# The feed-forward down projection with moving weights in four column groups, row output on two queues, longer weight runs, and x on the second queue

## The chip, the core and the metric

The kernel runs on one core of one Trainium2 chip. The metric is the device time of one execution in microseconds (us); medians are over several executions. Each execution also leaves its span, from the first to the last instruction on the core, and one execution of each kernel is traced by the hardware profiler. Spans are printed to 0.1 us, so stage lengths that run to the end of the span are good to 0.05 us.

In the profile PE is TensorE (its matmuls; PEld its weight loads), DVE is VectorE, ACT ScalarE and SP SyncE. A q, as in SPq, marks what the engine's sequencer does, such as issuing a DMA. SBUF is the core's working memory, PSUM the memory that matmuls write to. A time "at clock 0.5" was taken while the granted TensorE clock was at half.

## The reference

Two tokens pass through one decoder layer: attention over the last 2048 positions of a cache with 32 heads of 192, then a gated feed-forward network. Nearly all bytes are the cache.

```python
x = A_x                                               # [2, 1, 640], bf16
h = x + attention(layernorm(x), k_cache, v_cache, wq, wo)   # 32 heads, window 2048, head size 192
n = layernorm(h)
h2 = h + (gelu(n @ w_gate) * (n @ w_up)) @ w_down     # w_gate, w_up [640, 1536], w_down [1536, 640]
```

## The kernel before

All big loads go through a ring of SBUF slots on SyncE's DMA queue, in the order of their use: K, V and the projections for 16 groups of heads (two pairs of K and V each), then w_gate, w_up and w_down. The parts that the change touches are these (cuts are marked):

```python
P.op("sp", lambda e: e.dma_start(xrow[0:2, :], A_x[:, 0, :]), W=["xrow"], dma="dx")   # x first, same queue
load_k(0)
# ... all other loads; the last ones are:
for key, w in (("wg", B_w_gate), ("wu", B_w_up)):
    load(key, 2 * NC5 * F, w.rearrange("(p c) f -> p c f", c=NC5), ...)
wd = B_w_down.rearrange("(f p) n -> p f n", p=128)            # runs of 640 bf16 = 1280 B
for i in range(3):
    load(("wd", i), 2 * 4 * D, wd[:, 4 * i:4 * i + 4, :], ...)

# ... attention; then
layernorm(hT, "hT", hnT, "hnT")                               # h is held transposed: [128, 5, 2]
# gate and up: weights stationary, two columns (the two tokens) move
ins = e.matmul(bank[:, 2 * f:2 * f + 2], lhsT=wv[:, c, 128 * f:128 * (f + 1)], rhs=hnT[:, c, :], ...)
# ... gelu on DVE and ACT, uT = gelu(gate) * up
# w_down: weights stationary with a stride of 5, two columns move, 3 x 20 matmuls
ins = e.matmul(m2[:, 2 * c:2 * c + 2], lhsT=wd[:, f, c:D:NC5], rhs=uT[:, 4 * i + f, :], ...)
dve(tt(yT[...], m2[...], hT[:, :, :], ALU.add), ...)          # y stays transposed
e.dma_start(out[:, 0, :].rearrange("b (p c) -> p b c", c=NC5), yT[:, :, :])   # 256 pieces of 10 B
```

## Time and profile before

| what | value |
|---|---|
| time | 305.16 us, median of 3 (304.79 to 305.4) |
| span of the traced run | 303.6 us |
| DMA rate while the cache streams | about 420 GB/s, engines 90% busy or more from slice 2 to 38 |
| output of the second layernorm ready (hnT) | 290.66 us |
| uT ready | 294.80 us |
| last w_down group may start | 297.92 us |
| output issued | 299.13 us, 4.47 us before the end of the span |

The first lines to read are three rows of the page's forty slices of the kernel before: the TensorE clock that was granted, the busy share of the DMA engines (both in tenths) and the rate.

```profile
PEclk9999979995798899798799999798579999998555
DMA  6999999999999999999999999999999999999980
GB/s 240 412 435 414 427 426 420 428 399 427 425 422 423 426 421 421 427 399 428 421 428 426 421 418 426 421 407 420 433 419 426 421 421 417 429 419 424 417 308 27
```

The middle of the kernel is bound by DMA and nothing in this change touches it. What can change is how soon the stream starts, and what follows its end. TensorE's clock is at half from the 38th slice on.

The end of the chain of waits of the kernel before (start, duration, what) says which work ended last:

```profile
274.65 23.22 DMA ring<-in_B_w_down_dram
297.88 0.04 issue
297.92 0.97 PE m L629 x20
298.90 0.02 issue
298.92 0.18 DVE yT L316
```

In this execution the last landing of w_down ended the kernel: PE waited for it, then did 20 matmuls, DVE added h, and the output left. The timeline of the same execution (start, duration, engine, line, operation, and in brackets the idle time before and what ended it) has the start and the final stages:

```profile
0.74 0.37 SPq L318 DMA_DIRECT2D xrow<-in_A_x_dram  x1
1.17 1.28 SPq L261 DMA_DIRECT2D ring<-in_A_k_cache_dram  x2
...
290.71 1.76 PE L606 MATMUL sps<-hnT,ring 128*128 128x2 bf16 x60 [0.85 <-DVE hnT L316]
292.75 1.76 PE L606 MATMUL ops<-hnT,ring 128*128 128x2 bf16 x60 [0.28 <-DMA ring<-in_B_w_up_dram]
294.62 0.18 DVE L316 TENSOR_TENSOR uT<-ops,ga 128x24 bf16<-128x24 f32 x1 [0.26 <-PE ops L606]
294.86 0.96 PE L629 MATMUL m<-uT,ring 128*128 128x2 bf16 x20 [0.35 <-DVE uT L316]
296.03 0.80 PE L629 MATMUL m<-uT,ring 128*128 128x2 bf16 x16 [0.21 <-DMA ring<-in_B_w_down_dram]
297.19 0.28 PE L629 MATMUL m<-uT,ring 128*128 128x2 bf16 x4 [0.37 <-issue]
297.92 0.96 PE L629 MATMUL m<-uT,ring 128*128 128x2 bf16 x20 [0.45 <-DMA ring<-in_B_w_down_dram]
299.13 0.39 SPq L637 DMA_DIRECT2D out_dram<-yT  x1
```

x's issue delays the first K by 0.43 us. Gate and up take 29 ns per matmul (1.76/60), the w_down matmuls 48 ns (0.96/20), all at clock 0.5.

### The profile page before, as it was taken

To read this page: it belongs to the slowest core of one execution; us is meant where nothing else is said; L and a number is where in the kernel's file an instruction comes from. 1 tells how busy PE (TensorE), PEld (TensorE's weight loads), DVE (VectorE), ACT (ScalarE), POOL (GpSimd) and SP (SyncE) were. 2 spreads that over 40 slices of the span, in tenths; PEclk is the share of its full clock that TensorE was granted. 3 is DMA by queue.
4 is the path that set the end of the run, shared out by engine and by line. 5 is a ranking of instruction groups with operands and counts; after the bars stand their busy time and mean duration, and the time that the engine had idled before them with its cause. 6 is when DMAs were issued, how large, how long until landed. Compare 5 with 4: busy or idle time off the path is not lost.

```text
span 303.6 us, 7058 instructions
## 1 busy us (share of the span) xinstructions
PE 235.6 (78%) x3169; PEld 190.1 (63%) x3169; DVE 130.5 (43%) x360; ACT 112.2 (37%) x138; POOL 3.2 (1%) x9
## 2 busy tenths in 40 slices
PE   2878798962999988791898979692799889796762
PEld 1737394932868675771867676671785858575662
DVE  5837263720345364341446454351252736453120
ACT  2336343630425263522336353432243644442000
POOL 4000000000000000000000000000000000000000
PEclk9999979995798899798799999798579999998555
DMA  6999999999999999999999999999999999999980
GB/s 240 412 435 414 427 426 420 428 399 427 425 422 423 426 421 421 427 399 428 421 428 426 421 418 426 421 407 420 433 419 426 421 421 417 429 419 424 417 308 27
DMA packets 16323, 122.76 MB, mean 404 GB/s; under 512 B 1698, under 2 KB 3236, under 8 KB 7844
## 3 DMA queue, kind: packets, MB, share of 16 engines
q1 hardware_dynamic: 16292, 122.30, 96.9%
q8 instruction: 25, 0.41, 0.6%
q14 instruction: 6, 0.05, 0.0%
HBM read 122.29 MB, written 0.00 MB: 403 GB/s over the span
## 4 chain that ended last, share of the span: by engine, by line
DMA 57%; PE 31%; SPq 5%; DVE 3%; ACT 1%; issue 1%
DMA ring<-in_A_k_cache_dram 49%; PE tps L427 19%; DMA ring<-in_B_w_down_dram 8%; SPq L261 5%; PE m L541 3%; PE sps L489 3%; PE m L556 2%; PE ops L527 1%; ACT eexp L502 1%; PE m L447 1%; PE m L468 1%; PE m L539 1%; DVE mx L494 1%; DVE ktr L439 1%; PE m L512 1%
## 5 line engine op out<-in xcount | busy, mean ns | idle before, releaser
L427 PE MATMUL tps<-identf,ring 128*128 128x128 f32 x768 | 109.5, 305 | 37.4 <-DMA ring<-in_A_k_cache_dram 33.2
L427 PEld LDWEIGHTS tps<-identf,ring 128*128 128x128 f32 x768 | 101.1, 161 | 42.4 <-DMA ring<-in_A_k_cache_dram 34.0
L436 ACT ACTIVATE ktr<-tps 128x1024 bf16<-128x1024 bf16 x80 | 79.6, 1023 | 77.4 <-PE tps L427 77.4
L439 DVE COPY ktr<-tps 128x1024 bf16<-128x1024 bf16 x112 | 73.7, 688 | 47.3 <-PE tps L427 45.4
L489 PE MATMUL sps<-ktr,rq 128*32 128x512 bf16 x384 | 46.5, 631 | 0.7 <-DVE rq L316 0.5
L535 ACT ACTIVATE osb<-ops 128x384 f32<-128x384 f32 x16 | 7.9, 491 | 71.5 <-PE ops L527 71.5
L494 DVE TENSOR_REDUCE mx<-sps 128x1 f32<-128x512 f32 x16 | 11.1, 692 | 49.4 <-PE sps L489 49.4
L527 PEld LDWEIGHTS ops<-ring,ering 128*32 128x32 bf16 x1024 | 22.9, 101 | 10.5 <-issue 9.0
L527 PE MATMUL ops<-ring,ering 128*32 128x192 bf16 x1024 | 28.5, 255 | 0.2 <-DMA ring<-in_A_v_cache_dram 0.2
L489 PEld LDWEIGHTS sps<-ktr,rq 128*32 128x32 bf16 x384 | 10.9, 108 | 21.9 <-issue 21.0
L502 ACT ACTIVATE eexp<-sps,nm 128x1024 bf16<-128x1024 f32 x16 | 17.8, 1114 | 12.7 <-DVE nm L500 12.7
L541 PE MATMUL m<-sel,osb 128*128 128x2 f32 x96 | 19.4, 318 | 0.0
L541 PEld LDWEIGHTS m<-sel,osb 128*128 128x128 f32 x96 | 18.6, 269 | 0.0
L556 PEld LDWEIGHTS m<-ot,ring 128*128 128x128 bf16 x240 | 11.8, 129 | 1.1 <-DVE ot L316 1.1
L312 DVE TENSOR_SCALAR zrhs<-oh_b,zr 128x2 f32<-128x2 f32 x16 | 3.7, 229 | 20.4 <-ACT eexp L502 20.4
L556 PE MATMUL m<-ot,ring 128*128 128x2 bf16 x240 | 11.6, 177 | 0.9 <-DVE ot L316 0.9
L316 DVE TENSOR_TENSOR ering<-m,bmask 128x128 bf16<-128x128 f32 x16 | 11.3, 709 | 1.9 <-PE m L512 1.3
L498 PEld LDWEIGHTS m<-mrhs,pm 128*128 128x128 f32 x32 | 4.8, 188 | 11.5 <-DVE mrhs L312 11.5
L498 PE MATMUL m<-mrhs,pm 128*128 128x4 f32 x32 | 6.2, 263 | 7.1 <-DVE mrhs L312 7.1
L316 DVE TENSOR_TENSOR rq<-m,mask 128x24 bf16<-128x24 f32 x64 | 7.2, 175 | 9.6 <-PE m L468 9.6
L468 PE MATMUL m<-identb,qrow 2*128 2x2 bf16 x192 | 7.2, 159 | 4.6 <-DVE hT L316 3.7
L468 PEld LDWEIGHTS m<-identb,qrow 2*128 2x128 bf16 x192 | 5.8, 92 | 6.3 <-DVE hT L316 4.8
(84 smaller groups left out, 85.4 us busy)
## 6 DMA issues: line engine op xcount, KB each, us to landing
ring<-in_A_k_cache_dram SPq DMA_DIRECT2D x32, 1536.0 KB, 24.2
ring<-in_A_v_cache_dram SPq DMA_DIRECT2D x32, 1536.0 KB, 24.7
ring<-in_A_wq_dram SPq DMA_DIRECT2D x4, 1920.0 KB, 23.7
ring<-in_A_wo_dram SPq DMA_DIRECT2D x16, 480.0 KB, 19.7
ring<-in_B_w_gate_dram SPq DMA_DIRECT2D x1, 1920.0 KB, 27.4
ring<-in_B_w_up_dram SPq DMA_DIRECT2D x1, 1920.0 KB, 22.4
ring<-in_B_w_down_dram SPq DMA_DIRECT2D x3, 640.0 KB, 23.7
xrow<-in_A_x_dram SPq DMA_DIRECT2D x1, 2.5 KB
```

The costliest lines, as they stand in the source:

```text
L261: P.op("sp", lambda e, v=v, src=src: e.dma_start(v, src), W=toks + [("sem", i % NSEM)], dma=f"d{i % NSEM}")
L316: return lambda e: e.tensor_tensor(out=out, in0=a, in1=b, op=op)
L427: ins = e.transpose(tps[bi][:, 128 * u:128 * (u + 1)], kv[:, off:off + 128], identf[:, :])
L436: act(lambda e, dst=dst, bv=bv: e.activation(out=dst, in_=bv, func=ACT.Copy), W=[("kt", slot, bank)], X=[("t", bi)])
L439: dve(lambda e, dst=dst, bv=bv: e.tensor_copy(dst, bv), W=[("kt", slot, bank)], X=[("t", bi)])
L468: ins = e.matmul(m1[:, col:col + 2], lhsT=qx[:, h, o:o + 255:2], rhs=identb[p0:p0 + 2, p0:p0 + 2], start=True, stop=True, tile_position=(p ...
L489: ins = e.matmul(sps[32 * j:32 * (j + 1), :], lhsT=rq[:, g % 2, j, k, :], rhs=r, start=(k == 0), stop=(k == 5), tile_position=(0, 32 * j))
L494: dve(lambda e: e.tensor_reduce(out=mx[:, :], in_=sps[:, :], axis=AX.X, op=ALU.max), W=["mx"], X=["s"])
L502: act(lambda e: e.activation(out=eexp[:, :].rearrange("p (x d) -> p x d", d=2), in_=sps[:, :].unsqueeze(2).to_broadcast([128, 512, 2]), fu ...
L527: ins = e.matmul(ops_[32 * r:32 * (r + 1), 192 * h:192 * (h + 1)], lhsT=ering[:, g % 2, h, t, :], rhs=vv[:, DH * t:DH * (t + 1)], start=(h ...
L541: ins = e.matmul(m1[:, 32 + 2 * kk:34 + 2 * kk], lhsT=osb[:, kk:384:3], rhs=sel[:, :], start=True, stop=True)
L556: ins = e.matmul(m1[:, 48 + 2 * c:50 + 2 * c], lhsT=wo[:, kk, c:D:NC5], rhs=ot[:, kk, :], start=(kk == 0 and c == 0), stop=(kk == 2), skip ...
```

## The change

The intent is to shorten both ends. x goes to ScalarE's queue, so that K is issued first. In w_down the weights become the moving operand: uT's two columns stay in the array, four column groups of the array each take 160 of the 640 output columns, and y comes out as rows. So the output is 4 pieces of 320 B for each token, one token per queue. The residual h is turned into rows on PE (`h_rows`) and accumulated in the same PSUM bank. w_down is loaded in 4 chunks with several rows of w_down per partition, in runs of 5120 B (the two last chunks 2560 B). That permutes the hidden units, so gate and up must read their weights with a stride of 4 elements.

```diff
+WDC = ((0, 4), (4, 8), (8, 10), (10, 12))
-            wd = B_w_down.rearrange("(f p) n -> p f n", p=128)
-            for i in range(3):
-                load(("wd", i), 2 * 4 * D, wd[:, 4 * i:4 * i + 4, :], lambda v: ...)
+            wd = B_w_down.rearrange("(i p s) n -> i p s n", p=128, s=4)
+            for i, (f0, f1) in enumerate(WDC):
+                load(("wd", i), 2 * (f1 - f0) * D, wd[f0 // 4, :, f0 % 4:f0 % 4 + f1 - f0, :], lambda v: ...)
-        P.op("sp", lambda e: e.dma_start(xrow[0:2, :], A_x[:, 0, :]), W=["xrow"], dma="dx")
+        P.op("act", lambda e: e.dma_start(xrow[0:2, :], A_x[:, 0, :]), W=["xrow"], dma="dx")
+        dve(lambda e: e.tensor_copy(hTb[:, :, :], hT[:, :, :]), R=["hT"], W=["hTb"])      # behind the layernorm
-      e.matmul(bank[:, 2 * f:2 * f + 2], lhsT=wv[:, c, 128 * f:128 * (f + 1)], rhs=hnT[:, c, :],
+      e.matmul(bank[:, 2 * f:2 * f + 2], lhsT=wv[:, c, 512 * (f // 4) + f % 4:512 * (f // 4) + 512:4], rhs=hnT[:, c, :],
+        def h_rows(e):                                                                    # between gate and up
+            for c in range(NC5):
+                for r in range(4):
+                    ins = e.matmul(m1[32 * r:32 * r + 2, 128 + c:288:NC5], lhsT=hTb[:, c, :],
+                                   rhs=identb[:, 32 * r:32 * r + 32], start=(c == 0), stop=False, tile_position=(0, 32 * r), ...)
-                        ins = e.matmul(m2[:, 2 * c:2 * c + 2], lhsT=wd[:, f, c:D:NC5], rhs=uT[:, 4 * i + f, :], ...)
+                    for r in range(4):
+                        ins = e.matmul(m1[32 * r:32 * r + 2, 128:288], lhsT=uT[:, f, :],
+                                       rhs=wd[:, f - f0, 160 * r:160 * (r + 1)], start=False, stop=(f == NF - 1),
+                                       tile_position=(0, 32 * r), ...)
-        dve(tt(yT[...], m2[...], hT[:, :, :], ALU.add), ...)
-        P.op("sp", lambda e: e.dma_start(out[:, 0, :].rearrange("b (p c) -> p b c", c=NC5), yT[:, :, :]), ...)
+        dve(lambda e: e.tensor_copy(yrow[0:98, :], m1[0:98, 128:288]), W=["y"], X=["m1"])
+        for b, q in ((0, "sp"), (1, "act")):
+            P.op(q, lambda e, b=b: e.dma_start(out[b, 0, :].rearrange("(r n) -> r n", r=4), yrow[b:b + 97:32, :]), ...)
```

(Shapes, waits and the declarations of the new tiles are cut, and parts of lines where ... stands.)

## The prediction

> **What bounds it.** The 40 slices show the DMA engines 90% busy or more from slice 2 to 38 at about 420 GB/s; the chain of waits is 57% DMA: the cache stream sets the time. Only its two ends can change. In the timeline SyncE issues x first (0.74 to 1.11 us), K at 1.17. At the end, the last V is used at 282.35; then the engines run in turn: output projection, layernorm (hnT ready 290.66), gate 290.71 to 292.47, up 292.75 to 294.5, uT 294.80, three w_down groups, the last waiting for its DMA until 297.92, PE done 298.88, add 0.18, output issued 299.13, landed about 4.1 us later (tile view), span 303.6. The granted clock is 0.5 from about 278 on.
>
> **Start.** With x on ScalarE, K is issued about 0.4 us earlier (x's issue took 0.37). The stream and the final chain should move with it: -0.4.
>
> **w_down's DMA.** The last windows give about 355 GB/s at full share for 1280 B runs, against 420 for the cache. Longer runs should end the last landing 0.5 us sooner, plus 0.4: about 297.0. Worth little, because PE will be the later one.
>
> **Gate and up get slower.** Their stationary operand becomes a stride of 4 bf16. At clock 0.5, contiguous weights took 29 ns per matmul (1.76/60), stride-5 weights (old w_down) 48 ns (0.96/20). Score matmuls, whose moving operand has stride 4, took about twice the time per column of q_rows' contiguous ones. The Trainium skill (TensorE: Matmul & The Clock Gate, Weight-path perf modes) says fast weight load reads weights 32 bits at a time; strided bf16 would lose half, which fits. I estimate 48 ns for stride 4: gate +1.15, up +1.15, on the chain behind the last V. Up's 0.28 us wait for w_up disappears.
>
> **h_rows** adds 20 small matmuls between gate and up: +0.5 us (estimate, 25 ns each). The hTb cast hides under gate.
>
> **w_down on PE.** 48 matmuls of 160 columns, four column groups at once. pv did 32 of 192 columns in 1.47 us at this clock; scaled, about 1.8 us in one piece, without a DMA wait. uT comes at 294.8 + 2.5 = 297.3, PE ends at 299.1: 0.25 later, before the shift.
>
> **Copy.** 160 fp32 columns from PSUM instead of 10: about 0.33 instead of 0.18, +0.15.
>
> **Output.** 256 pieces of 10 B become 4 of 320 B on each of two queues. [...]The skill (DMA: Bandwidth & Descriptors, Anatomy of one DMA) puts most of the fixed cost on the target memory's write receipt, so some stays: estimate 2.7 from issue instead of 4.2, -1.5.
>
> **Sum:** -0.4 + 0.25 + 0.15 - 1.5 = -1.5 us. From 305.16: 303.7 us, 8 in 10 between 302.4 and 304.8. Chances: faster by over 2% 0.01, within 2% 0.98, slower 0.01; 2% is 6.1 us, more than the ends hold.
>
> **What would show it:** first K issue near 0.75 us; gate and up 2.9 us each; no DMA wait before a w_down group; w_down in one run of 1.8 us; output landing under 3 us after issue.
>
> **What would make it wrong:** stride-4 weights as fast as contiguous ones (then w_down's DMA binds and 1 us more is won); the denser final stretch raising the clock to 1.0 (PE shorter by 2 us); write receipts no quicker for 320 B than for 10 B (1.5 lost); a later start of the stream because two queues share the engines.

## The result and the profile after

The changed kernel takes 303.39 us, median of 4 runs (302.67 to 304.06), against 304.98 for the kernel before (304.61 to 305.4, 4 runs). The ratio is 0.9943, 95% interval 0.9923 to 0.9964: 0.6% less. Ratios here are the mean time of one kernel's fast runs over the mean of the other's of the same rounds, so they are not quite the ratio of the medians. The traced run's span is 301.1 us.

The end of the chain of waits after the change:

```profile
239.48 22.83 DMA ring<-in_A_k_cache_dram
262.31 0.04 issue
262.36 4.51 PE tps L430 x24
...
291.42 2.16 PE sps L610 x60
293.58 0.37 PE m L627 x20
293.95 2.11 PE ops L610 x60
...
296.39 0.70 PE m L641 x14
297.09 0.12 issue
297.21 1.26 PE m L641 x32
298.47 0.02 issue
298.49 0.33 DVE yrow L647
```

No w_down landing ends the kernel any more: from the landing of a K tile (the 31st of 32, called K 30 below) the chain runs through PE, DVE and ACT alone. The timeline lines that answer to those before:

```profile
0.73 1.31 SPq L263 DMA_DIRECT2D ring<-in_A_k_cache_dram  x2
0.74 0.55 ACTq L321 DMA_DIRECT2D xrow<-in_A_x_dram  x1
...
291.42 2.16 PE L610 MATMUL sps<-hnT,ring 128*128 128x2 bf16 x60 [0.85 <-DVE hnT L319]
293.51 0.44 PE L627 MATMUL m<-identb,hTb 128*2 128x32 bf16 x20
293.88 2.16 PE L610 MATMUL ops<-hnT,ring 128*128 128x2 bf16 x60
296.15 0.18 DVE L319 TENSOR_TENSOR uT<-ops,ga 128x24 bf16<-128x24 f32 x1 [0.68 <-PE ops L610]
296.39 2.06 PE L641 MATMUL m<-ring,uT 128*2 128x160 bf16 x48 [0.34 <-DVE uT L319]
298.49 0.33 DVE L647 CAST yrow<-m 98x160 bf16<-98x160 f32 x1 [2.16 <-PE m L641]
298.85 0.66 SPq L649 DMA_DIRECT2D out_dram<-yrow  x1
298.85 0.61 ACTq L649 DMA_DIRECT2D out_dram<-yrow  x1
```

By stage, from these two traces (us):

| stage | before | after | change |
|---|---|---|---|
| hnT ready at | 290.66 | 291.36 | +0.70 |
| hnT to uT (gate, h_rows, up) | 4.14 | 4.97 | +0.83 |
| uT to the start of the last DVE step (w_down) | 4.12 | 2.16 | -1.96 |
| last DVE step to the output's issue | 0.21 | 0.36 | +0.15 |
| issue to the end of the span | 4.47 | 2.25 | -2.22 |
| span | 303.6 | 301.1 | -2.50 |

The sum is close to what was predicted, but two things don't fit. hnT came 0.7 us later although the stream starts 0.43 us sooner. And the span lost 2.5 us while the time lost about 1.6. Over the runs of one later session the gap is the same: mean span 303.50 before and 300.95 after (-2.55), mean time 305.38 and 303.48 (-1.90).

### The profile page after: what moved, and what is told of

The parts are those of the page before. It is cut to its first block, busy times and chain, and to the rows that moved or that the text cites. A ratio compares the mean times of both kernels' runs of the same rounds, so it can differ in the third digit from the quotient of the medians.

```text
span 301.1 us, 7078 instructions
## 1 busy us (share of the span) xinstructions
PE 236.2 (78%) x3177; PEld 191.2 (64%) x3177; DVE 130.4 (43%) x361; ACT 112.2 (37%) x138; POOL 3.2 (1%) x9
## 4 chain that ended last, share of the span: by engine, by line
DMA 48%; PE 39%; DVE 7%; ACT 3%; SPq 2%; issue 1%; POOL 0%; ACTq 0%; POOLq 0%; DVEq 0%
DMA ring<-in_A_k_cache_dram 48%; PE tps L430 20%; PE sps L492 4%; PE m L544 4%; PE ops L530 2%; PE m L559 2%; SPq L263 2%; ACT eexp L505 2%; PE m L450 1%; DVE mx L497 1%; PE m L542 1%; PE m L471 1%; DVE ktr L442 1%; PE sps L610 1%; PE ops L610 1%
## 5 line engine op out<-in xcount | busy, mean ns | idle before, releaser
L559 PEld LDWEIGHTS m<-ot,ring 128*128 128x128 bf16 x240 | 11.8, 129 | 1.1 <-DVE ot L319 1.1
L559 PE MATMUL m<-ot,ring 128*128 128x2 bf16 x240 | 11.7, 177 | 0.9 <-DVE ot L319 0.9
```

Source lines behind the costliest of these rows:

```text
L559: ins = e.matmul(m1[:, 48 + 2 * c:50 + 2 * c], lhsT=wo[:, kk, c:D:NC5], rhs=ot[:, kk, :], start=(kk == 0 and c == 0), stop=(kk == 2), skip ...
```

## The experiments

Twelve kernels ran, all with correct results. In each session the kernel before ran beside them; ratios are to it.

### A second look at both kernels, and where the late layernorm came from

`after_again` and `before_again` are the two kernels unchanged.

> The kernel after, unchanged, as a control on the same chip and for a second trace. If the late final chain of the first trace (24 transposes at clock 0.5 after the landing of K 30, 4.51 us against 2.84) is the luck of the clock windows, another trace shows those windows elsewhere and the layernorm output ready at another time, between 290.2 and 291.4 us; if it belongs to the change, the same 24 transposes are slow again. Time 303.4 us, ratio 0.994.

> The kernel before, unchanged, for a second trace: where its half-clock windows fall near the landing of K 30 (24 transposes in 2.84 us at full clock in the first trace), when its layernorm output is ready (290.66 in the first), and whether it pauses before the same 3146th matmul. If the slow transposes of the changed kernel are luck of the windows, either can appear here; ratio 1.000.

`after_again`: 303.47 us (302.49 to 304.25, 6 runs), ratio 0.9940 (0.9923 to 0.9956): the result is repeated. `before_again`: one look, 306.01 us, span 304.1.

The traces show that the time of hnT varies in both kernels from one execution to the next. PE transposes K 30 in 24 matmuls as soon as it lands; the timelines have them in four executions, first of the kernel before,

```profile
262.74 2.84 PE L427 MATMUL tps<-identf,ring 128*128 128x128 f32 x24 [1.32 <-DMA ring<-in_A_k_cache_dram]
```

then of `before_again`,

```profile
263.15 5.38 PE L427 MATMUL tps<-identf,ring 128*128 128x128 f32 x24 [3.06 <-DMA ring<-in_A_k_cache_dram]
```

and of the kernel after, whose second trace (`after_again`) has 4.13 us.

```profile
262.36 4.51 PE L430 MATMUL tps<-identf,ring 128*128 128x128 f32 x24 [2.73 <-DMA ring<-in_A_k_cache_dram]
```

The same work takes 2.84 us at full clock and 5.38 us at half clock. The clock record of the traces changes only in steps of 3.41 us. The Trainium skill (TensorE: Matmul & The Clock Gate, Part 1) says the same, a free-running window of 3413 ns; it adds that its phase does not start with the kernel, which would fit how the half-clock window falls on these 24 matmuls in one execution and misses them in another. hnT was ready at 290.66 and 292.46 us in the two traces of the kernel before, at 291.36 and 290.43 in the two of the kernel after. So +0.70 in the table can't be put down to the change: slow transposes appear in both kernels, and the fast ones (2.84 us) in one of the two traces of the kernel before and in two variants of the changed kernel below (`short_runs`, `early_shift_s2`). Nor do these 24 matmuls decide hnT alone: `after_again` has slow ones (4.13 us) and still the earlier hnT, because a full-clock window from 284.05 to 287.46 us fell on the last group's matmuls, which the first trace ran at half clock (L542 to the start of L559: 1.86 us against 2.30). What I can't say from two traces per kernel is whether the change makes the slow windows more or less frequent.

### The start: x alone on ScalarE's queue

```diff
-        P.op("sp", lambda e: e.dma_start(xrow[0:2, :], A_x[:, 0, :]), W=["xrow"], dma="dx")
+        P.op("act", lambda e: e.dma_start(xrow[0:2, :], A_x[:, 0, :]), W=["xrow"], dma="dx")
```

> The kernel before, with nothing but x moved to the ScalarE queue. Theory A (the start is worth its 0.4 us): K is issued near 0.74 us instead of 1.17, the slowest landing of the last V and the last w_down landing come about 0.4 us earlier, and the time falls by about 0.4 us (ratio 0.9987). Rival B (the shift is lost to the clock windows and the PE chain of the last K): landings move, the end does not, ratio 1.000 within 0.0007.

304.94 us (304.28 to 305.07, 5 runs), ratio 0.9983 (0.9971 to 0.9995), which is 0.5 us of 305.4. In its trace the last landing of w_down came at 297.3 us against 297.9 in the kernel before, and the output was issued at 298.85 against 299.13. Theory A is the better fit: the start is worth about 0.5 us in this kernel, where the landing still mattered. The interval is wide (0.15 to 0.9 us), and its low end touches rival B's band.

### The output: size of the pieces, and the second queue

`out_10B` keeps everything of the changed kernel but cuts each row into pieces of 10 B, by leaving a gap in SBUF after every fifth element (the copy into yrow, cut here, leaves the same gaps):

```diff
-        yrow = sb("yrow", [128, 160], BF16)
+        yrow = sb("yrow", [128, 32, 6], BF16)
-        e.dma_start(out[b, 0, :].rearrange("(r n) -> r n", r=4), yrow[b:b + 97:32, :])
+        e.dma_start(out[b, 0, :].rearrange("(r j c) -> r j c", r=4, c=5), yrow[b:b + 97:32, :, 0:5])
```

> The kernel after, with each output piece cut to 10 B (an SBUF row of 6 elements per piece, 5 used), still 2 queues of 4 rows. Theory A (the size of the pieces sets the landing): from issue to the end rises from 2.2 us to 4 us or more, time +1.5 to +2 us. Rival B (the second queue, or the final write alone, was the gain): no more than +0.4 us.

305.78 us (304.78 to 306.44, 6 runs), ratio 1.0014 (0.9999 to 1.003). This gives back all of the change's gain: 2.3 us over `after_again` of the same session. From issue to the end of the span it takes 4.89 us, against 2.43 in `after_again`; everything ahead of it was equal (issue at 298.31 and 298.27). So the gain in the output stage is the size of the pieces, and with it their number (256 instead of 8), which can't be varied alone. The kernel before had 4.47 and 4.60 us with the same 10 B, spread over 128 partitions.

`one_queue` sends both rows from SyncE:

```diff
-        for b, q in ((0, "sp"), (1, "act")):
+        for b, q in ((0, "sp"), (1, "sp")):
```

> The kernel after with both output rows on SyncE. The issue of one row took 0.66 us, so the second row should be issued 0.66 us later and the span end about 0.6 us later: time +0.6 us, of the 2.2 us that the output stage won. If the sequencer's issue were hidden, no change.

303.95 us (303.28 to 304.42, 4 runs), ratio 0.9942 (0.9925 to 0.9958). The time cannot tell 0.6 us here, as the interval is 1 us wide and this run's w_down had no pause (below). The trace can: the two issues took 1.27 us in a row and the stage 2.8 us, where the nine traces with both queues and pieces of 320 B have 2.22 to 2.43. The second queue is worth about 0.5 us of the stage.

### The weights' stride and the length of the runs

`short_runs` undoes the new layout of w_down alone, so that gate and up read contiguous weights; `stride2` is the half step, two rows per partition. (The slices that go with the new layouts are cut.)

```diff
 short_runs:
-            wd = B_w_down.rearrange("(i p s) n -> i p s n", p=128, s=4)
+            wd = B_w_down.rearrange("(f p) n -> p f n", p=128)
-   lhsT=wv[:, c, 512 * (f // 4) + f % 4:512 * (f // 4) + 512:4]
+   lhsT=wv[:, c, 128 * f:128 * (f + 1)]
 stride2:
+            wd = B_w_down.rearrange("(j p s) n -> p j (s n)", p=128, s=2)
+   lhsT=wv[:, c, 256 * (f // 2) + f % 2:256 * (f // 2) + 256:2]
```

> The kernel after, with w_down loaded as before (1280 B runs, still 4 chunks) and so gate and up with contiguous weights. Theory A (PE is the later one at the end of the changed kernel, and the stride costs 0.4 us in each of gate and up): gate and up fall from 2.16 to 1.76 us each, the span falls by up to 0.8 us, limited by the w_down landing, which comes about 0.5 us later: net 0.0 to -0.6 us against the changed kernel. Rival B (longer runs are what wins): the last w_down group waits for its DMA again and the time is 0.5 us over the changed kernel.

> The kernel after with w_down in runs of 2560 B (2 rows per partition) and so gate and up with weights of stride 2 instead of 4. Measured so far at clock 0.5: stride 1 29 ns per matmul, stride 4 36, stride 5 48. If only the bytes spanned count, stride 2 stands near 29 to 31 ns: gate and up about 1.8 us each, span 0.3 to 0.7 us under the changed kernel. If any stride breaks the fast load, 36 ns and no change.

`short_runs`: 303.87 us (303.24 to 304.7, 6 runs), ratio 0.9958 (0.9945 to 0.9971). `stride2`: 303.98 us (303.93 to 304.17, 5 runs), ratio 0.9947 (0.9934 to 0.9960). Neither is faster than the changed kernel. But gate and up did become faster, as the timeline of `stride2` shows:

```profile
291.17 1.76 PE L610 MATMUL sps<-hnT,ring 128*128 128x2 bf16 x60 [0.85 <-DVE hnT L319]
292.86 0.43 PE L627 MATMUL m<-identb,hTb 128*2 128x32 bf16 x20
293.23 1.76 PE L610 MATMUL ops<-hnT,ring 128*128 128x2 bf16 x60
295.33 0.70 PE L641 MATMUL m<-ring,uT 128*2 128x160 bf16 x16 [0.34 <-DVE uT L319]
297.47 1.23 PE L641 MATMUL m<-ring,uT 128*2 128x160 bf16 x32 [1.43 <-issue]
```

All at clock 0.5, per matmul: stride 1 29 ns, stride 2 29 ns, stride 4 36 ns (2.16/60), stride 5 48 ns (w_down before). From start to start, without the end of the last matmul, these are 27, 27, 34 and 41 ns, and the output projection's matmuls, also of stride 5, are 41 ns apart too. So stride 4 costs 0.4 us in each of gate and up, not the 1.15 that was predicted from stride 5, and stride 2 costs nothing. About 0.3 us of each miss is the quotient: 60 matmuls at 41 instead of 27 ns would have been +0.84, not +1.15.

The 0.8 us saved went into the last line: 1.43 us of idle time before the 17th w_down matmul, ended by nothing that the profile names. `short_runs` has the same 1.43 us at the same matmul. Its profile blames a w_down chunk, but its chain has that chunk landing at 295.46, then a full microsecond of "issue", and PE going on at 296.46. The length of the runs, by contrast, moves the last landing little: 296.8 to 297.1 us in the traces with long runs, 297.1 in `short_runs`.

### h_rows out of the way

`hrows_early` casts h on ScalarE and puts the 20 matmuls into the layernorm, where PE waits for DVE.

```diff
-        dve(lambda e: e.tensor_copy(hTb[:, :, :], hT[:, :, :]), R=["hT"], W=["hTb"])
+        act(lambda e: e.activation(out=hTb[:, :, :], in_=hT[:, :, :], func=ACT.Copy), R=["hT"], W=["hTb"])
+        # in the layernorm, behind its first matmul (its old place behind gate is taken out):
+        pe(h_rows, R=["hTb", "identb"], X=["m1"])
```

> The kernel after with the cast of h on ScalarE and the 20 h_rows matmuls inside the layernorm, where PE waits for VectorE, instead of between gate and up. If PE's chain sets the end of the changed kernel, the 0.37 us between gate and up go and the output is issued 0.37 us earlier, time -0.3 to -0.4. If the end is set by the w_down landing or by the pause inside the w_down matmuls (0.1 to 0.5 us, ended by nothing that the profile names), the gap grows instead and the time stays.

303.64 us (302.87 to 304.08, 6 runs), ratio 0.9931 (0.9918 to 0.9944). hnT to uT fell from 4.97 to 4.51 us, as it should, and the pause in w_down grew to 0.58 us. Against the changed kernel (0.9940, 0.9943) it is not clearly faster: mostly the second alternative.

### The pause: an instruction fetch

Everything that made PE faster ended in the same pause. It always lies at the same place of PE's program. The kernel before has 3169 matmuls and pauses 24 before the end; the changed one has 3177 and pauses 32 before the end. Both are behind the 3145th matmul, although in one it is the 36th of w_down and in the other the 16th. And in the traces' list of DMA packets one instruction packet of 16 KB starts 2.4 to 2.6 us before PE goes on:

| run | packet starts | PE goes on | between | pause |
|---|---|---|---|---|
| before | 294.66 | 297.19 | 2.53 | 0.37 |
| before_again | 295.74 | 298.17 | 2.43 | 0.13 |
| x_only | 294.94 | 297.52 | 2.58 | 0.83 |
| after | 294.84 | 297.21 | 2.37 | 0.12 |
| after_again | 294.26 | 296.63 | 2.37 | 0.47 |
| out_10B | 294.27 | 296.67 | 2.40 | 0.48 |
| hrows_early | 294.47 | 296.94 | 2.47 | 0.58 |
| stride2 | 294.94 | 297.47 | 2.53 | 1.43 |
| short_runs | 293.98 | 296.46 | 2.48 | 1.43 |

(`one_queue`: packet at 294.81, no pause; its uT came late, and the 17th matmul was not due before 297.4.) The Trainium skill (Runtime: NRT & Kernel Launch, Instruction fetch mechanics) says that instructions come in blocks of 16 KiB, 256 of them. A matmul here is two instructions, its weight load and itself, so a block is 128 matmuls. The page also says that crossing a block costs little and is mostly hidden. To test it, `fetch_shift` adds 112 matmuls in the middle, at group 5, where PE has time:

```diff
+            if g == 5:
+                pe(lambda e: [e.matmul(m1[:, 60:62], lhsT=identb[:, :], rhs=identb[:, 0:2], start=True, stop=True)
+                              for _ in range(112)][-1], R=["identb"], X=["m1"])
```

> The kernel after with 112 tiny matmuls (2 columns, unused result) added at pair 5, where PE waits for the cache anyway. In all traces so far PE pauses before its 3146th matmul of the unchanged or changed program, whatever that matmul is (36 into w_down before, 16 into it after), about 2.4 us after a 16 KB instruction packet starts. Theory: the pause is the instruction fetch. Then with 112 more matmuls the pause before the 17th w_down matmul is gone or moves to another matmul, 112 earlier or 126 later; the w_down matmuls run in one piece of about 1.9 us; time 0 to -0.5 us. Rival: the pause belongs to w_down's second chunk (a late landing): it stays before the 17th w_down matmul.

303.59 us (303.49 to 304.29, 5 runs), ratio 0.9936 (0.9924 to 0.9949), so no clear gain. The timeline of `fetch_shift` in w_down:

```profile
296.21 1.24 PE L644 MATMUL m<-ring,uT 128*2 128x160 bf16 x32 [0.34 <-DVE uT L319]
298.22 0.70 PE L644 MATMUL m<-ring,uT 128*2 128x160 bf16 x16 [0.77 <-issue]
```

The pause left the 17th matmul and stands before the 33rd: 16 later, which is 128 - 112. The packet started at 295.73, again 2.49 us before PE went on. The 33rd matmul uses the third chunk, which had landed at 296.1. The rival, a late second chunk, is out; the pause follows the instruction count: 112 matmuls more, and it is 128 later. One coincidence has to be looked at: in this run the fourth chunk landed late, at 298.19, just before PE went on. But the code lets the 33rd to 40th matmul wait for the third chunk alone, and in `early_shift` below PE did go on with them at 297.73, before its fourth chunk landed at 298.31. So w_down did not run in one piece, as the expectation had it; the pause only moved.

The next step was to put the block's end where it can't hurt. With h_rows early and 92 added matmuls one block ends at gate's 44th matmul, whose fetch can run during the layernorm, and the next one behind the last matmul of all. (The edits are those of `hrows_early` and `fetch_shift` together.) `early_shift` does that with the changed kernel's stride of 4, `early_shift_s2` with stride 2 and runs of 2560 B, `early_shift_short` with contiguous weights and runs of 1280 B.

> h_rows inside the layernorm as in hrows_early, and 92 tiny matmuls at pair 5, so that by the count seen so far (the pause falls before the 3146th matmul and every 128 on either side) the pauses fall at about gate's 44th matmul, whose fetch can run during the layernorm, and behind the last w_down matmul. Theory: no pause in gate, up or w_down; w_down runs 1.8 to 1.9 us in one piece unless a chunk is late; the output is issued 0.5 to 0.6 us earlier than in hrows_early for the same layernorm time; time -0.3 to -0.6 us against the changed kernel. Rival (the pause is not the fetch): it stays inside w_down.

> early_shift and also w_down in runs of 2560 B with weights of stride 2. stride2 alone saved 0.4 us in each of gate and up and gave it all back in a longer pause (1.43 us). Without the pause the saving should show, until the last w_down landing (about 297.1) binds: PE done about 0.4 us after it, time -0.6 to -1.0 us against the changed kernel.

> The same with 1280 B runs and contiguous weights. Gate and up as in early_shift_s2 (1.76 us each measured for both strides); what differs is the w_down landing, 0.0 to 0.3 us later by the traces so far. If the w_down landing now binds, this is up to 0.3 us slower than early_shift_s2; if it does not, they are equal.

| run | time, us | ratio (95%) |
|---|---|---|
| early_shift | 303.44 (303.24 to 303.65, 6 runs) | 0.9928 (0.9915 to 0.9940) |
| early_shift_s2 | 303.31 (303.1 to 303.64, 6 runs) | 0.9924 (0.9912 to 0.9936) |
| early_shift_short | 303.61 (303.38 to 303.85, 6 runs) | 0.9933 (0.9919 to 0.9947) |

The pause is gone in all three, as expected, and yet w_down did not end sooner. The timeline of `early_shift_s2`:

```profile
290.39 1.76 PE L622 MATMUL sps<-hnT,ring 128*128 128x2 bf16 x60 [0.85 <-DVE hnT L319]
292.43 1.76 PE L622 MATMUL ops<-hnT,ring 128*128 128x2 bf16 x60 [0.28 <-DMA ring<-in_B_w_up_dram]
294.54 0.70 PE L645 MATMUL m<-ring,uT 128*2 128x160 bf16 x16 [0.34 <-DVE uT L319]
297.08 1.23 PE L645 MATMUL m<-ring,uT 128*2 128x160 bf16 x24 [1.84 <-DMA ring<-in_B_w_down_dram]
298.67 0.43 PE L645 MATMUL m<-ring,uT 128*2 128x160 bf16 x8 [0.35 <-DMA ring<-in_B_w_down_dram]
```

PE was ready at 294.5 and then waited twice for w_down, whose last landing came at 298.6 instead of 296.8 to 297.1. Each load lands in 16 parts. In `early_shift_s2` 15 of the 16 parts of the last chunk had landed at 297.11 and the last one at 298.62; in `early_shift` the two numbers are 297.18 and 298.31, in `early_shift_short` 297.32 and 298.69, in `fetch_shift` 296.87 and 298.19. In the changed kernel, without added matmuls, they are 296.91 and 296.99. The lag appears with the load that was under way when the last instruction packet ran: in `fetch_shift` the third chunk still shows 0.11 us between its last two parts, then the packet starts at 295.73, and the fourth shows 1.32.

Why this packet and not the last one of the other kernels? Counting the 16 KB packets of its queue in all fourteen traces gives a pattern. In every trace the loads in flight after the 9th and the 17th packet have a last part that is 0.9 to 1.5 us behind the one before it; after the 8th, 16th and 24th that gap is 0.32 us or less. The added matmuls pull the 9th packet from 117 to 120 us forward to 110 to 113 us, and the lag comes forward with it. Listed part by part (in `after` and `early_shift_s2`), nearly every packet drops one more part back, and that part stays back. So the parts fall behind in rounds of eight packets, and each new round raises the distance from a load's first part to its last:

| first to last part of a load, us | before and after the 9th packet | the 17th | the 25th |
|---|---|---|---|
| after | 1.74, 2.97 | 3.42, 4.59 | none before the last landing |
| fetch_shift | 1.88, 3.21 | 3.50, 4.87 | 5.00, 6.25 |
| early_shift_s2 | 2.02, 3.53 | 3.59, 5.09 | 5.05, 6.48 |

The ten traces without added matmuls have 24 such packets before the last landing of w_down; the four with them have 25. The 92 or 112 added matmuls, most of a block, thus brought a 25th packet, the first of a fourth round, in front of the last loads, and that cost the 1.1 to 1.5 us. Which DMA engine carries which packet the trace doesn't say, nor why the rounds have eight. That a program with fewer instructions would let the stream land earlier is what this suggests; it was not tried.

### The time outside the span

There is one more piece. In six traced runs (`after_again`, `short_runs`, `out_10B`, `stride2`, `hrows_early`, `one_queue`) a further 16 KB instruction packet starts between 1.8 and 1.9 us after the last instruction of the span. In these runs the time is 2.57 to 2.98 us longer than the span. In the other seven with a known time (`before_again`, `x_only`, `after`, `fetch_shift` and the three `early_shift` kernels) there is none, and the difference is 1.78 to 2.11 us. No run of either group lies in the other's range. Over all runs of a kernel the difference averages 1.9 us in `x_only`, 2.5 in `after_again`, and 1.77 to 1.86 in the `early_shift` kernels. This accounts for a span that fell by 2.55 us and a time that fell by 1.90: in most of its runs the changed kernel pays about 0.65 us more after its last instruction. In the three `early_shift` kernels, whose blocks' ends were moved, it is gone. That the packet is the cause is likely from this, but no run isolates it.

So no version clearly beats the changed kernel. `early_shift_s2` has the lowest ratio, 0.9924 (0.9912 to 0.9936) against 0.9940 (0.9923 to 0.9956); the intervals overlap, and the two stand against different sessions on different chips. The expectation of -0.6 to -1.0 us was missed. It wins the pause, the stride and the time outside the span, and loses 1.5 us to the late landing.

## Why the prediction was right

The forecast was 303.7 us and the measured time 303.39, inside the range of 302.4 to 304.8, and "within 2%" had 0.98. The reason given for the small size holds: the cache stream fills the kernel and only its ends can change. Term by term:

- **Start, -0.4.** Right. K was issued at 0.73 us, and `x_only` measured a ratio of 0.9983, -0.5 us. The text also said that the final chain would move by it; in most traces it did not visibly, because half-clock windows, at K 30 and behind it, move hnT by more than that (290.1 to 292.5 us over all traces).
- **w_down's landing at about 297.0.** Right: 296.99 in the first trace. The part put down to longer runs (0.5 us) was too large: `short_runs` landed at 297.1, and `x_only`, with the old loads, at 297.3. So the number was right in part by scatter: the traces of the kernel before landed at 297.88 and 298.10.
- **Gate and up, +1.15 each.** The direction was right and the size wrong. Stride 4 takes 36 ns per matmul and not 48, so +0.4 each; part of the 48 was the end of the last matmul in a short block. The reading that "strided bf16 would lose half" failed: stride 2 costs nothing, and 48 ns belongs to stride 5.
- **h_rows, +0.5.** 0.37 to 0.46 us.
- **w_down on PE, 1.8 us in one piece.** The matmuls do take 1.77 us where they run in one piece (`one_queue`). In the other unshifted traces they are cut by a fetch pause of 0.12 to 1.43 us. That was not foreseen, though a line of the profile before showed it.
- **Copy, +0.15.** Measured +0.15.
- **Output, -1.5.** Measured -2.2 in the first pair of traces; `out_10B` shows that the 10 B pieces were the cause (4.89 against 2.43 us). The mechanism was right and the size too small: by the semaphores the later row landed 1.85 us after its issue instead of the estimate of 2.7, against 4.08 before. What remains, 2.22 to 2.43 us to the end of the span, was not taken apart.
- **The sum.** On the span the terms give -2.5 instead of -1.5. About 0.65 us of that is paid again after the last instruction, which no term had. So the total of -1.6 to -1.9 is near the forecast partly because an underrated gain met an unforeseen cost. The chain on PE was luck as well: its end was forecast at 298.7 (299.1 less the shift) and came at 298.47, but hnT came 1.1 us later than forecast, hnT to uT took 1.7 us less (4.97 instead of 6.64), and w_down 0.3 us more, with its pause.

What the result does not settle is how much of the 0.83 us of gate, h_rows and up is really lost to the end. As `stride2` and `short_runs` show, as long as the pause stands behind it, PE time saved ahead of it comes to nothing.

## What to carry to other kernels

In a kernel that is bound by its DMA stream, ask of each edit which end it touches, and cost the last write by the size of its pieces: rows of 320 B landed about 2.5 us sooner than pieces of 10 B. When a chain of small matmuls ends a program, count PE's instructions: a pause that the profile calls "issue" and that always comes at the same instruction may be a fetch (add instructions far ahead and see whether it moves), and a faster engine ahead of it only waits longer. Added instructions are not free: here they brought one more instruction packet in front of the last loads, and the landing was 1.1 to 1.5 us later. Compare stages over more than one trace before believing a difference, because a half-clock window of 3.4 us can move a stage by 1 to 2 us in either kernel.

## What the Trainium skill lacked or had wrong

- Runtime: NRT & Kernel Launch, Instruction fetch mechanics: it says that crossing a 16 KiB block is mostly hidden. Here, in the small matmuls at the end of a full DMA stream, PE waited 0.12 to 1.43 us at the end of a block, and went on 2.37 to 2.58 us after the packet started. Its 256 instructions per block agree with the runs (112 added matmuls moved the pause to 128 matmuls later, each with its weight load).
- No page has that 16 KB instruction packets (about 1.06 us each) set the parts of a running stream back one after another: in all fourteen traces the last of the 16 parts fell 0.9 to 1.5 us behind the others after the 9th and the 17th packet, and after the 25th in the four traces where it came before the last landing. Nor that a packet fetched behind the last instruction goes with 0.5 to 1.2 us more of measured time outside the span.
- TensorE: Matmul & The Clock Gate, Weight-path perf modes: it names packed and strided reads of fast weight load without a different cost. At clock 0.5 the matmuls with 128 x 128 bf16 weights started 27 ns apart at stride 1 and 2, 34 at stride 4, 41 at stride 5; no run shows whether fast weight load was on.
- DMA: Bandwidth & Descriptors, Anatomy of one DMA: it has a fixed cost of about 2 us for DMAs issued from GpSimd. The 320 B output, issued from SyncE and ScalarE, landed 1.84 to 1.94 us after its issue (the later row, in the nine traces with two queues), which is close; no run shows the write receipt by itself. No page has a time for a write of 256 pieces of 10 B: here 3.88 to 4.39 us.
